# Loading q and k in 32-token blocks and transposing them on VectorE from the third batch on

## The chip, the cores and the metric

The kernel runs on one core of a Trainium2 chip. The metric is the device time of one execution in microseconds (us). Engines are named as in the profile: PE is TensorE's matmuls and PEld its weight loads, DVE is VectorE, ACT is ScalarE, POOL is GpSimd, SP is SyncE, which here only issues DMAs.

## What is computed

For each of 8 batches and 8 heads, 32 pack vectors attend over 576 tokens; then the 576 queries attend over the 32 packed results. The attention output of all heads goes through two matrices with a softplus between them.

```python
scale = 1.0 / np.sqrt(q.shape[-1])           # q, k, v: (8, 8, 576, 64), p: (8, 8, 32, 64)
p_packed = sm_attn(p, k, v)                  # softmax(scale * p k^T) v
out = sm_attn(q, p_packed, p_packed)
x = out.transpose(0, 2, 1, 3).reshape(B * S, H * D)        # (4608, 512)
h = x @ w_in                                 # (512, 2048)
g = np.maximum(h, 0.0) + np.log1p(np.exp(-np.abs(h)))
result = (g @ w_out).astype(np.float32)      # (2048, 512)
```

## The kernel before

The work goes batch by batch. A batch has two groups `g` of four heads each, and its 576 tokens are handled in two halves `c` of 288 columns. The main loop (lines 620 to 671) runs over 128 units: a unit is one batch `b` and one of 16 slices `f` of 128 of the 2048 hidden columns. In each unit PE does `gemm1` (line 497: 12 matmuls into the two halves of `ph`), ACT and DVE make the softplus of it (lines 523 to 528) and split it into two parts `gh` and `gl` (513, 514), and two units later (`LAG`) PE does the second product (`gemm2_tile`, line 541: four tiles `acc` of three matmuls). At a batch's last slice each `acc` is copied by DVE to a tile `o` (550) and stored by SP (556); the last 64 tokens of two batches share a tile `acc_m` with 48 further matmuls. There are two banks for `ph`, so the `gemm1` of the next unit overwrites them as soon as the softplus's last reader, line 528 on DVE, is through.

The attention of batch b+1 is a generator, `attention`, that is stepped 0.56 times after each of a unit's four `gemm2` tiles (`PACE`), so that its pieces lie between the matmuls of batch b. PE's order is as written; a scheduler places the other engines' instructions. The pieces that matter here:

- `load` (112 to 122) brings q, k or v of one batch and group by one DMA of SP into a tile of 96 partitions: partition x holds the six tokens 6x to 6x+5 of each head, runs of 1536 bytes. The pool `ld` has four tiles; a load waits until the tile of four loads before is read to its end.
- `transposed` (234 to 246) turns one head of k or q so that its 64 dimensions lie on the partitions: three transposes on PE into a PSUM bank `psT` (line 239), and one ACT copy of 128 x 288 to the tile `T` (line 245). Two tokens are turned at once, so that rows 0 to 63 of `T` hold the tokens of one half and rows 64 to 127 those of the other. There are 16 such calls in a batch.
- `scores1` and `scores2` (line 252) multiply by `T`; `a1` (261) and `at_h`, `at_l` (442, 443) take the results, the two halves next to each other. So the tokens stand in another order than in memory, the same in all steps; `packed` (295) picks v to match, and `store` undoes it with two DMAs for each tile of 128 rows.
- `scores2`'s result goes through DVE: 32 x 32 transposes (319, 343) around a softmax over 32 columns (lines 327 to 340).

Of the kernel before, what the change touches and what calls it, by code (L numbers as in the profile page):

```python
# [26 lines left out]
def pack_attention_then_softplus_ffn(  # L27
# [10 lines left out]
    nc = tc.nc  # L38
# [13 lines left out]
    LAG = 2  # L52
    MC = 512
# [58 lines left out]
    def load(nm, b, g):  # L112
        if b >= B:
            return
        t = ld.tile([NP, HG, SI, D], F32, tag="ld", name=f"{nm}_{b}_{g}")
        nc.sync.dma_start(
            t.rearrange("x h s d -> x h (s d)"),
            {"q": q, "k": k, "v": v}[nm][b, g * HG:(g + 1) * HG].rearrange(
                "h (x s) d -> x h (s d)", s=SI
            ),  # L120
        )
        loaded[nm, b, g] = t
# [111 lines left out]
    def transposed(nm, b, g, hh):  # L234

        src = loaded[nm, b, g]
        ps = bank(f"psT_{nm}_{b}_{g}_{hh}")
        for i in range(HS):
            nc.tensor.transpose(  # L239
                ps[:, i * NP:(i + 1) * NP],  # L240
                src[:, hh, 2 * i:2 * i + 2, :].rearrange("x s d -> x (s d)"),
                ident[:NP, :NP],
            )
        dst = work.tile([P, C], F32, tag="T", name=f"T_{nm}_{b}_{g}_{hh}", bufs=4)
        nc.scalar.copy(dst, ps[:, :C])  # L245
        return dst
# [10 lines left out]

    def scores1(b, g, c, kT, a1):
        cols = slice(b % BG * J, (b % BG + 1) * J)
        ps = scores(1, b, g, c, lambda hh: pT[:, g * HG + hh, cols], kT)  # L260
        nc.scalar.copy(a1[:, c * C:(c + 1) * C], ps)
# [28 lines left out]
    def packed(b, g, a1T, rs):  # L290

        ps = bank(f"psp_{b}_{g}")
        for s in range(SI):
            for hh in range(HG):
# [3 lines left out]
                    loaded["v", b, g][:, hh, 2 * (s % HS) + s // HS, :],  # L298
# [134 lines left out]
    def weights(b):  # L433
# [4 lines left out]
        for c in range(2):  # L438
            cols = slice(c * C, (c + 1) * C)
            for g in range(G):  # L440
                aT = res[b]["aT"][g, c]
                nc.scalar.copy(at_h[:, g, cols], aT)
                nc.vector.tensor_tensor(  # L443
                    at_l[:, g, cols], aT, at_h[:, g, cols].bitcast(F32), op=ALU.subtract
                )
# [100 lines left out]
    outv = [out[b * S:(b + 1) * S, :].rearrange("(x s) e -> s x e", s=SI) for b in range(B)]  # L546

    def store(acc, pieces, nm):
        o = cv.tile([P, DM], F32, tag="x", name=f"o_{nm}", bufs=2)
        nc.vector.tensor_copy(o, acc)  # L550
        for row, b, col, n in pieces:
            while n:
                i, x = divmod(col, NP)
                m = min(n, NP - x)
                s = i % HS * 2 + i // HS
                nc.sync.dma_start(outv[b][s, x:x + m, :], o[row:row + m, :])
# [144 lines left out]
```

## Time and profile before

| what | value |
|---|---|
| runs of the kernel | 799.79, 796.33 and 799.0 us; median 799.0 |
| profiled execution, first to last instruction (span) | 794.2 us; its own time is not listed beside it |
| PE busy | 766.6 us (97%) |
| DVE busy | 511.3 us (64%) |
| ACT busy | 464.8 us (59%) |
| POOL busy | 94.2 us (12%) |
| DMA queue of SP | 37,600 packets, 54.93 MB, 27.2% of 16 engines |
| chain that ended last | PE 80%, and all else under 1% each |

The span is that of one profiled execution and the runs are others; the median of the runs is 4.8 us above the span, the fastest run 2.1 us. The busy share of an engine is its mean over the span. "Chain" is the work followed back from the last instruction, at each step to what released it.

### The profile page before, as it was taken

Reading aid. Unit: us, or ns where it says so; the run is one execution under the profiler, and the core shown is the slowest. Engines: PE = TensorE matmul, PEld = TensorE weight load, DVE = VectorE, ACT = ScalarE, POOL = GpSimd, SP = SyncE. Lnnn points to the kernel's source line nnn. Section 1 sums busy time; section 2 is a strip of 40 time slices with the busy share of each in tenths; the row PEclk is TensorE's granted clock in tenths of the full one; section 3 lists DMA queues with packets and bytes.
Section 4 is the critical chain, followed back from the end, with each engine's and each line's share of the span. In section 5 each row is a group of like instructions: output and inputs, shape, how many; then the busy total and the mean of one; then the engine's idle time right before and its main releaser. Section 6 shows DMA issues by size and latency. Waiting matters only on the chain.

```text
span 794.2 us, 14986 instructions
## 1 busy us (share of the span) xinstructions
PE 766.6 (97%) x5724; PEld 609.0 (77%) x5724; DVE 511.3 (64%) x1168; ACT 464.8 (59%) x1181; POOL 94.2 (12%) x166
## 2 busy tenths in 40 slices
PE   6879988999999999999999999999999999999997
PEld 4656766877788787877788787887888777778886
DVE  2788899754686547765677447764677546765554
ACT  5769887665662755665554555665555465555540
POOL 1415353000000000000000000000000000000010
PEclk9999999999999999999999999999999999999999
DMA  9977784031213121032213112132211210010002
GB/s 229 248 188 178 172 229 112 8 107 31 61 31 83 45 56 48 18 83 61 61 31 84 26 50 60 31 84 61 61 31 42 56 31 2 1 54 1 1 0 67
DMA packets 38216, 56.02 MB, mean 71 GB/s; under 512 B 4864, under 2 KB 31488, under 8 KB 38144
## 3 DMA queue, kind: packets, MB, share of 16 engines
q1 hardware_dynamic: 37600, 54.93, 27.2%
q8 instruction: 45, 0.74, 0.4%
q14 instruction: 27, 0.22, 0.1%
q10 hardware_dynamic: 544, 0.13, 0.1%
HBM read 45.61 MB, written 9.44 MB: 69 GB/s over the span
## 4 chain that ended last, share of the span: by engine, by line
PE 80%; ACT 0%; DVE 0%; issue 0%; ACTq 0%; DVEq 0%
PE acc L541 40%; PE ph L497 23%; PE acc_m L541 6%; PE psm L460 3%; PE ps L252 2%; PE psT_q L239 2%; PE psT_k L239 2%; PE psp L295 1%; PE psa L285 1%; PE psx L308 0%; PE ppt L105 0%; ACT e L525 0%; ACT e L524 0%; ACT e L523 0%; DVE o L550 0%; DVE o_m L550 0%
## 5 line engine op out<-in xcount | busy, mean ns | idle before, releaser
L528 DVE SCALAR_TENSOR_TENSOR e<-ph,e 128x288 f32<-128x288 f32 x256 | 114.5, 454 | 167.5 <-ACT e L525 166.2
L541 PE MATMUL acc<-wo_h,gh 128*128 128x512 f32 x512 | 214.8, 419 | 0.7 <-DVE o L550 0.7
L541 PE MATMUL acc<-wo_l,gh 128*128 128x512 f32 x512 | 201.6, 394 | 0.0
L541 PE MATMUL acc<-wo_h,gl 128*128 128x512 f32 x512 | 201.5, 394 | 0.0
L523 ACT ACTIVATE e<-ph 128x288 f32<-128x288 f32 x256 | 103.0, 403 | 163.1 <-PE ph L497 110.7
L497 PE MATMUL ph<-at_h,mh 128*128 128x288 f32 x512 | 159.0, 311 | 5.4 <-DVE e L528 4.5
L497 PE MATMUL ph<-at_l,mh 128*128 128x288 f32 x512 | 152.2, 297 | 1.4 <-DVE at_l L443 1.2
L497 PE MATMUL ph<-at_h,ml 128*128 128x288 f32 x512 | 152.2, 297 | 0.0
L497 PEld LDWEIGHTS ph<-at_h,mh 128*128 128x128 f32 x512 | 96.8, 189 | 40.0 <-DVE gl L514 14.1
L534 POOL COPY rest<-e 128x64 f32<-128x64 f32 x128 | 47.3, 369 | 599.3 <-DVE e L528 598.5
L541 PEld LDWEIGHTS acc<-wo_h,gh 128*128 128x128 f32 x512 | 96.4, 188 | 23.1 <-issue 9.8
L541 PEld LDWEIGHTS acc<-wo_h,gl 128*128 128x128 f32 x512 | 96.4, 188 | 21.7
L524 ACT ACTIVATE e<-e 128x288 f32<-128x288 f32 (+1 forms) x240 | 109.2, 455 | 3.5
L525 ACT ACTIVATE e<-e 128x288 f32<-128x288 f32 (+1 forms) x240 | 109.7, 457 | 2.0
L541 PEld LDWEIGHTS acc<-wo_l,gh 128*128 128x128 f32 x512 | 96.9, 189 | 9.8
L497 PEld LDWEIGHTS ph<-at_l,mh 128*128 128x128 f32 x512 | 97.0, 189 | 4.5 <-DVE at_l L443 2.3
L497 PEld LDWEIGHTS ph<-at_h,ml 128*128 128x128 f32 x512 | 96.9, 189 | 0.0
L514 DVE TENSOR_TENSOR gl<-e,gh 128x512 fp32r<-128x512 f32 x128 | 88.0, 688 | 6.9 <-DVE gh L513 0.5
L513 DVE CAST gh<-e 128x512 fp32r<-128x512 f32 x128 | 57.8, 452 | 6.2
L475 ACT CAST mh<-psm 128x512 fp32r<-128x512 f32 (+1 forms) x72 | 35.5, 541 | 41.2 <-PE psm L460 40.8
L476 DVE TENSOR_TENSOR ml<-psm,mh 128x512 fp32r<-128x512 f32 (+1 forms) x72 | 42.7, 622 | 21.8 <-ACT mh L475 21.7
L460 PE MATMUL psm<-w_in_sb,pt 64*32 64x512 f32 (+1 forms) x576 | 38.6, 553 | 6.3 <-ACT T_q L245 2.1
(75 smaller groups left out, 816.7 us busy)
## 6 DMA issues: line engine op xcount, KB each, us to landing
k<-in_k SPq DMA_DIRECT2D x16, 576.0 KB, 4.6
v<-in_v SPq DMA_DIRECT2D x16, 576.0 KB, 4.5
q<-in_q SPq DMA_DIRECT2D x16, 576.0 KB, 4.9
x_i<-in_moe_w_in SPq DMA_DIRECT2D x32, 256.0 KB, 5.9
x_o<-in_moe_w_out SPq DMA_DIRECT2D x16, 512.0 KB, 3.7
out<-o SPq DMA_DIRECT2D x24, 192.0 KB, 2.5
out<-o SPq DMA_DIRECT2D x16, 128.0 KB, 2.4
out<-o SPq DMA_DIRECT2D x24, 64.0 KB, 2.8
```

The costliest lines, as they stand in the source:

```text
L460: nc.tensor.matmul(ps[hh * J:(hh + 1) * J, :n], res["pt"][g][o:o + D, hh * J:(hh + 1) * J], w_in_sb[o:o + D, hh, c * n:(c + 1) * n], start ...
L475: nc.scalar.copy(mh[:, cols], ps[:, :n])
L476: nc.vector.tensor_tensor(ml[:, cols], ps[:, :n], mh[:, cols].bitcast(F32), op=ALU.subtract)
L497: nc.tensor.matmul(ph[:, :C], x[:, ms], y[:, g, cs], start=(i == 0), stop=(i == 3 * G - 1),)
L513: nc.vector.tensor_copy(hi, x)
L514: nc.vector.tensor_tensor(lo, x, hi.bitcast(F32), op=ALU.subtract)
L523: nc.scalar.activation(es[c], hv[c], AF.Abs)
L524: nc.scalar.activation(e[:, x], e[:, x], AF.Exp, scale=-1.0)
L525: nc.scalar.activation(e[:, x], e[:, x], AF.Ln, bias=1.0)
L528: nc.vector.scalar_tensor_tensor(es[c], hv[c], 0.0, es[c], op0=ALU.max, op1=ALU.add)
L534: nc.gpsimd.tensor_copy(rest[:, rest_at(b, f), r:r + REST], e[:, NT * P:])
L541: nc.tensor.matmul(acc, x[:, cs], y[:, f, :], start=(first and i == 0), stop=(last and i == 2),)
```

## The change

The constant `BY_BLOCK` is 2: batches 0 and 1 stay as they are, and batches 2 to 7 keep their tokens in the order of memory. There a tile of q or k has 128 partitions and is loaded by four DMAs, one for 32 partitions each: a partition gets 4 heads x 9 blocks x 32 numbers, and the runs in memory are 32 numbers (128 bytes). Partitions 0 to 63 take the even blocks of 32 tokens, 64 to 127 the odd ones, and two neighbouring groups of 32 partitions the two halves of the 64 dimensions. One VectorE instruction, a transpose of 32 x 32 blocks of the whole 128 x 288, then makes the tile `T` from SBUF; PE's three transposes, the PSUM bank and ACT's copy are gone. A tile of v is loaded by one DMA in runs of 64 numbers (256 bytes) instead of 384 (1536 bytes). The copies to `a1`, `at_h` and `at_l` write blocks of 32 columns with a step of 64 (`half`, `by_half`), and the result of a tile of 128 rows is stored by one DMA.

```diff
--- before.py
+++ after.py
@@ -50,6 +50,8 @@
     NT = S // P
     REST = S - NT * P
     LAG = 2
+    BY_BLOCK = 2
+    NB = C // J
     MC = 512
     scale = 1.0 / math.sqrt(D)
 
@@ -112,13 +114,25 @@
     def load(nm, b, g):
         if b >= B:
             return
-        t = ld.tile([NP, HG, SI, D], F32, tag="ld", name=f"{nm}_{b}_{g}")
-        nc.sync.dma_start(
-            t.rearrange("x h s d -> x h (s d)"),
-            {"q": q, "k": k, "v": v}[nm][b, g * HG:(g + 1) * HG].rearrange(
-                "h (x s) d -> x h (s d)", s=SI
-            ),
-        )
+        src = {"q": q, "k": k, "v": v}[nm][b, g * HG:(g + 1) * HG]
+        if b < BY_BLOCK:
+            t = ld.tile([NP, HG, SI, D], F32, tag="ld", name=f"{nm}_{b}_{g}")
+            nc.sync.dma_start(
+                t.rearrange("x h s d -> x h (s d)"), src.rearrange("h (x s) d -> x h (s d)", s=SI)
+            )
+        elif nm == "v":
+            t = ld.tile([NP, HG, SI, D], F32, tag="ld", name=f"{nm}_{b}_{g}")
+            nc.sync.dma_start(
+                t.rearrange("x h s d -> x (h s) d"), src.rearrange("h (s x) d -> x (h s) d", s=SI)
+            )
+        else:
+            t = ld.tile([P, HG, NB, J], F32, tag="ld", name=f"{nm}_{b}_{g}")
+            blocks = src.rearrange("h (n c x) (w d) -> c w x (h n) d", c=2, x=J, w=D // J)
+            for o in range(P // J):
+                c, w = divmod(o, D // J)
+                nc.sync.dma_start(
+                    t[o * J:(o + 1) * J].rearrange("x h n d -> x (h n) d"), blocks[c, w]
+                )
         loaded[nm, b, g] = t
 
     CN = 512
@@ -234,6 +248,10 @@
     def transposed(nm, b, g, hh):
 
         src = loaded[nm, b, g]
+        if b >= BY_BLOCK:
+            dst = work.tile([P, C], F32, tag="T", name=f"T_{nm}_{b}_{g}_{hh}", bufs=4)
+            nc.vector.transpose(dst, src[:, hh].rearrange("x n d -> x (n d)"))
+            return dst
         ps = bank(f"psT_{nm}_{b}_{g}_{hh}")
         for i in range(HS):
             nc.tensor.transpose(
@@ -255,10 +273,22 @@
             )
         return ps[:, :C]
 
+    def half(b, c, x):
+
+        if b < BY_BLOCK:
+            return x[:, c * C:(c + 1) * C]
+        return x.rearrange("p (n c x) -> p c n x", c=2, x=J)[:, c]
+
+    def by_half(b, x):
+        return x if b < BY_BLOCK else x.rearrange("p (n x) -> p n x", x=J)
+
+    def copy_half(b, c, copy, dst, src):
+        copy(half(b, c, dst), by_half(b, src))
+
     def scores1(b, g, c, kT, a1):
         cols = slice(b % BG * J, (b % BG + 1) * J)
         ps = scores(1, b, g, c, lambda hh: pT[:, g * HG + hh, cols], kT)
-        nc.scalar.copy(a1[:, c * C:(c + 1) * C], ps)
+        copy_half(b, c, nc.scalar.copy, a1, ps)
 
     def softmax1_max(b, g, a1):
         m = small.tile([P, 1], F32, tag="m1", name=f"m1_{b}_{g}", bufs=1)
@@ -295,7 +325,7 @@
                 nc.tensor.matmul(
                     ps[hh * J:(hh + 1) * J, :D],
                     a1T[:, s, hh * J:(hh + 1) * J],
-                    loaded["v", b, g][:, hh, 2 * (s % HS) + s // HS, :],
+                    loaded["v", b, g][:, hh, 2 * (s % HS) + s // HS if b < BY_BLOCK else s, :],
                     start=(s == 0), stop=(s == SI - 1),
                 )
         pp = small.tile([P, 2, D], F32, tag="pp", name=f"pp_{b}_{g}", bufs=1)
@@ -436,12 +466,12 @@
         at_l = work.tile([P, G, S], F32R, tag="at_l", name=f"at_l_{b}", bufs=1)
         res[b]["at"] = (at_h, at_l)
         for c in range(2):
-            cols = slice(c * C, (c + 1) * C)
             for g in range(G):
                 aT = res[b]["aT"][g, c]
-                nc.scalar.copy(at_h[:, g, cols], aT)
+                copy_half(b, c, nc.scalar.copy, at_h[:, g], aT)
                 nc.vector.tensor_tensor(
-                    at_l[:, g, cols], aT, at_h[:, g, cols].bitcast(F32), op=ALU.subtract
+                    half(b, c, at_l[:, g]), by_half(b, aT), half(b, c, at_h[:, g].bitcast(F32)),
+                    op=ALU.subtract,
                 )
 
 
@@ -543,17 +573,24 @@
                 start=(first and i == 0), stop=(last and i == 2),
             )
 
-    outv = [out[b * S:(b + 1) * S, :].rearrange("(x s) e -> s x e", s=SI) for b in range(B)]
+    outb = [out[b * S:(b + 1) * S, :] for b in range(B)]
+
+    def rows_of(b, col):
+
+        if b >= BY_BLOCK:
+            return outb[b][col:]
+        i, x = divmod(col, NP)
+        s = i % HS * 2 + i // HS
+        return outb[b].rearrange("(x s) e -> s x e", s=SI)[s, x:]
 
     def store(acc, pieces, nm):
         o = cv.tile([P, DM], F32, tag="x", name=f"o_{nm}", bufs=2)
         nc.vector.tensor_copy(o, acc)
         for row, b, col, n in pieces:
             while n:
-                i, x = divmod(col, NP)
-                m = min(n, NP - x)
-                s = i % HS * 2 + i // HS
-                nc.sync.dma_start(outv[b][s, x:x + m, :], o[row:row + m, :])
+                to = rows_of(b, col)
+                m = min(n, to.shape[0])
+                nc.sync.dma_start(to[:m], o[row:row + m, :])
                 row, col, n = row + m, col + m, n - m
 
     def rests(b):
```

What moves on DVE, the main loop of batch 4 with the attention of batch 5 in it. In the names, `a_5_0_1` is the second score of batch 5, group 0, half 1; `T_q_1_0` is head 0 of group 1 of q; `e_10` is the softplus of unit 10. Before, from the first transpose of group 0's scores to the softplus of unit 10:

```order
L319 STREAM_TRANSPOSE a_5_0_0_5942<-ps_5_0_0_5937 128x288
L327 TENSOR_REDUCE m_5_0_0_5980<-a_5_0_0_5942 128x9
L319 STREAM_TRANSPOSE a_5_0_1_5949<-ps_5_0_1_5944 128x288
L328 TENSOR_TENSOR a_5_0_0_5942<-a_5_0_0_5942,m_5_0_0_5980 128x288
L327 TENSOR_REDUCE m_5_0_1_6062<-a_5_0_1_5949 128x9
L328 TENSOR_TENSOR a_5_0_1_5949<-a_5_0_1_5949,m_5_0_1_6062 128x288
L336 TENSOR_REDUCE z_5_0_0_5998<-a_5_0_0_5942 128x9
L528 SCALAR_TENSOR_TENSOR e_10_5965<-ph_10_0_5951,e_10_5965 128x288
```

and now:

```order
L349 STREAM_TRANSPOSE a_5_0_0_5748<-ps_5_0_0_5743 128x288
L253 STREAM_TRANSPOSE T_q_1_0_5798<-q_1_5386 128x288
L349 STREAM_TRANSPOSE a_5_0_1_5755<-ps_5_0_1_5750 128x288
L357 TENSOR_REDUCE m_5_0_0_5786<-a_5_0_0_5748 128x9
L253 STREAM_TRANSPOSE T_q_1_1_5858<-q_1_5386 128x288
L358 TENSOR_TENSOR a_5_0_0_5748<-a_5_0_0_5748,m_5_0_0_5786 128x288
L357 TENSOR_REDUCE m_5_0_1_5860<-a_5_0_1_5755 128x9
L253 STREAM_TRANSPOSE T_q_1_2_5871<-q_1_5386 128x288
L558 SCALAR_TENSOR_TENSOR e_10_5771<-ph_10_0_5757,e_10_5771 128x288
```

Three of the four transposes of q's group 1 come in ahead of unit 10's first line 528 (now 558), and two instructions of the softmax have moved behind it.

Further on in the same batch, before, from the second maximum of group 1's scores to unit 13's softplus:

```order
L327 TENSOR_REDUCE m_5_1_1_6188<-a_5_1_1_6142 128x9
L328 TENSOR_TENSOR a_5_1_0_6135<-a_5_1_0_6135,m_5_1_0_6155 128x288
L328 TENSOR_TENSOR a_5_1_1_6142<-a_5_1_1_6142,m_5_1_1_6188 128x288
L336 TENSOR_REDUCE z_5_1_0_6192<-a_5_1_0_6135 128x9
L337 TENSOR_SCALAR z_5_1_0_6192<-z_5_1_0_6192 128x9
L338 RECIPROCAL z_5_1_0_6192<-z_5_1_0_6192 128x9
L339 TENSOR_TENSOR a_5_1_0_6135<-a_5_1_0_6135,z_5_1_0_6192 128x288
L528 SCALAR_TENSOR_TENSOR e_13_6173<-ph_13_0_6159,e_13_6173 128x288
```

and now:

```order
L357 TENSOR_REDUCE m_5_1_1_5978<-a_5_1_1_5932 128x9
L358 TENSOR_TENSOR a_5_1_0_5925<-a_5_1_0_5925,m_5_1_0_5945 128x288
L358 TENSOR_TENSOR a_5_1_1_5932<-a_5_1_1_5932,m_5_1_1_5978 128x288
L253 STREAM_TRANSPOSE T_k_0_0_6146<-k_0_5502 128x288
L366 TENSOR_REDUCE z_5_1_0_5982<-a_5_1_0_5925 128x9
L253 STREAM_TRANSPOSE T_k_0_1_6159<-k_0_5502 128x288
L367 TENSOR_SCALAR z_5_1_0_5982<-z_5_1_0_5982 128x9
L253 STREAM_TRANSPOSE T_k_0_2_6196<-k_0_5502 128x288
L558 SCALAR_TENSOR_TENSOR e_13_5963<-ph_13_0_5949,e_13_5963 128x288
L368 RECIPROCAL z_5_1_0_5982<-z_5_1_0_5982 128x9
L366 TENSOR_REDUCE z_5_1_1_6000<-a_5_1_1_5932 128x9
```

Three of the four transposes of k for batch 6 stand ahead of unit 13's first line 558; the reciprocal and the product with it have moved behind it.

On SP, early in the main loop of batch 4, the stores of batch 3 and the load of q (group 0) for the attention of batch 5, before:

```order
L556 DMA out<-o_0_5286 96x512
L556 DMA out<-o_0_5286 32x512
L556 DMA out<-o_1_5293 64x512 x2
L116 DMA q_0_5425<-in_q 96x4x384
L556 DMA out<-o_2_5307 32x512
L556 DMA out<-o_2_5307 96x512
L556 DMA out<-o_3_5318 96x512
L556 DMA out<-o_3_5318 32x512
```

and now:

```order
L133 DMA q_0_5251<-in_q 32x36x32 x4
L593 DMA out<-o_0_5124 128x512
L593 DMA out<-o_1_5130 128x512
L593 DMA out<-o_2_5139 128x512
L593 DMA out<-o_3_5149 128x512
L593 DMA out<-o_m 64x512 x2
```

The load of q now stands as four DMAs ahead of the stores, where it stood between the second and the third tile, and each tile's store is one DMA.

## Rows read from the trace of the kernel before

**Rows 1.** Busy time by stretch: us, busy by engine (count), PEclk, DMA share, GB/s

```profile
427.00:524.00 97.00, 97.00 (x720) 77.52 (x718) 59.45 (x140) 52.41 (x141) 6.12 (x16) 1.00 0.19 51
524.00:610.00 86.00, 86.00 (x671) 68.53 (x670) 55.32 (x131) 52.22 (x140) 5.94 (x16) 1.00 0.21 55
```

**Rows 2.** Chain of waits from 160 to 700 us, shares by engine and line

```profile
by line: PE acc L541 49.5%; PE ph L497 29.1%; PE acc_m L541 6.1%; PE psm L460 4.5%; PE ps L252 2.9%; PE psT_q L239 2.2%; PE psT_k L239 2.0%; PE psp L295 1.8%; PE psa L285 1.5%; PE psx L308 0.2%; PE ppt L105 0.2%
```

**Rows 3.** Chain of waits from 427 to 524 us in order: start us, us, what

```profile
465.56 0.25 PE psT_q L239 x3
...
487.26 1.39 PE acc L541 x6
...
493.24 0.70 PE acc L541 x3
493.94 0.25 PE psT_q L239 x3
494.19 1.42 PE acc L541 x6
...
495.86 0.73 PE acc L541 x3
496.58 1.59 PE ph L497 x12
...
506.43 1.59 PE ph L497 x12
```

**Rows 4.** Groups, 160 to 700 us: line engine op operands count | busy us, mean ns | idle

```profile
L239 PE MATMUL psT_q<-ident,q 96*128 96x96 f32 x144 | 19.8, 245 | 0.0
...
L245 ACT COPY T_q<-psT_q 128x288 f32<-128x288 f32 x48 | 18.9, 394 | 22.1 <-PE psT_q L239 21.9
...
L239 PE MATMUL psT_k<-ident,k 96*128 96x96 f32 x132 | 18.1, 245 | 0.0
...
L245 ACT COPY T_k<-psT_k 128x288 f32<-128x288 f32 x44 | 17.5, 397 | 23.3 <-PE psT_k L239 22.8
...
L343 DVE STREAM_TRANSPOSE aT<-a 128x288 f32<-128x288 f32 x24 | 11.3, 471 | 0.2
...
L443 DVE TENSOR_TENSOR at_l<-aT,at_h 128x288 fp32r<-128x288 f32 x24 | 10.1, 460 | 0.8
```

**Rows 5.** Busy time in two stretches of 5 us, columns as in rows 1

```profile
489.00:494.00 5.00, 5.00 (x43) 3.44 (x42) 4.96 (x14) 3.39 (x10) 0.24 (x1) 1.00 0.00 0
504.00:509.00 5.00, 5.00 (x28) 4.38 (x27) 4.81 (x15) 3.47 (x11) 0.24 (x1) 1.00 0.02 5
```

**Rows 6.** VectorE in order, 485 to 509 us: start us, us, instruction [idle before <-releaser]

```profile
486.06 0.45 DVE L327 TENSOR_REDUCE m<-a 128x9 f32<-128x288 f32 x1
486.44 0.47 DVE L319 STREAM_TRANSPOSE a<-ps 128x288 f32<-128x288 f32 x1
486.83 0.42 DVE L328 TENSOR_TENSOR a<-a,m 128x288 f32<-128x288 f32 x1
...
494.16 0.46 DVE L528 SCALAR_TENSOR_TENSOR e<-ph,e 128x288 f32<-128x288 f32 x1 [0.15 <-ACT e L525]
495.05 0.46 DVE L528 SCALAR_TENSOR_TENSOR e<-ph,e 128x288 f32<-128x288 f32 x1 [0.44 <-ACT e L525]
...
505.23 0.45 DVE L528 SCALAR_TENSOR_TENSOR e<-ph,e 128x288 f32<-128x288 f32 x1
...
505.98 0.42 DVE L528 SCALAR_TENSOR_TENSOR e<-ph,e 128x288 f32<-128x288 f32 x1
```

**Rows 7.** DMA queue of the four p loads, 133 to 140 us: packets, MB, engine share

```profile
q1 hardware_dynamic: 1088, 0.26, 16.8%
```

**Rows 8.** The same of one v load, 202 to 207 us

```profile
q1 hardware_dynamic: 400, 0.59, 45.3%
```

**Rows 9.** SyncE's DMA issues in order: start us, us, what

```profile
427.31 2.44 SPq L556 DMA_DIRECT2D out<-o  x4
429.84 0.54 SPq L116 DMA_DIRECT2D q<-in_q  x1
```

## The prediction

> **What bounds the kernel now.** I first compared engines by stretch. The reader is to see that in the main loop, with batch 4's 97 us and batch 5's 86 us as examples, PE is busy all of the time at the full granted clock of 1.00 (the 2.4 GHz level), DVE 61 to 64%, ACT 54 to 61%, and the DMA engines about a fifth [rows 1]. The 11 us by which the two batches differ are the 48 matmuls of `acc_m`. Second, the chain of waits between 160 and 700 us: every share belongs to PE, so nothing waits there but for PE's own next matmul, and 4.2% of it are the transposes of q and k at line 239 [rows 2]. Whatever PE no longer has to do in this loop is won, up to the point where another engine comes too late.
>
> **What is removed from PE.** Batches 2 to 7 have 6 x 2 tensors x 2 groups x 4 heads = 96 calls of `transposed`, each three transposes on PE. Between 160 and 700 us there are 144 + 132 of them [rows 4], that is 92 calls; the other four lie shortly before 160. The chain gives 4.2% of 540 us = 22.7 us for 92 calls, 0.247 us each, as its rows in order of time show singly (0.25). All three take 0.25 us although one is listed with 245 ns, because they are pipelined. Around such a piece the matmuls run a little longer: three of `acc` take 0.73 us behind one and 0.70 in front of it, six take 1.42 behind one and 1.39 elsewhere [rows 3]. So a call costs PE 0.25 to 0.30 us; I take 0.27, one such loss of 0.03 being seen most times, though not each time. 96 x 0.27 = **25.9 us** off the path; the ends are 23.7 and 28.8.
>
> **What is removed from ACT.** 96 copies of 128 x 288 at 394 to 397 ns [rows 4], 38 us. ACT is not on the path, so this gives nothing by itself. The softplus's ACT steps come a little earlier, which I don't count.
>
> **What is added to DVE.** 96 transposes of 128 x 288 out of SBUF. The kernel has that very shape at line 343, 471 ns [rows 4]: 45 us in all, 7.5 us for a batch. A batch of 86 us becomes 81.7 (16 x 0.27 less), and DVE's 55.3 us [rows 1] become 62.8, 77%. On average that is covered by PE. It need not be covered in every place: before, DVE already had two dense stretches in each batch, busy 4.96 us of 5 and 4.81 of 5 [rows 5], where the softmax over the packs is done, and the order puts T_q of group 1 into the first and three T_k of the next batch into the second.
>
> In a dense stretch the price is less than 471 ns: instructions of 0.42 to 0.47 us start 0.38 and 0.39 us apart [rows 6], so I take 0.40 for each added one. The one who waits is `gemm1`, which needs a bank of `ph` back from line 528.
> - First stretch. Line 528 of unit 11 ran at 494.16 to 494.62 and 495.05 to 495.51 [rows 6], and unit 12's `gemm1` began at 496.58 [rows 3], its second half 0.79 us on (half of 1.59). Four transposes come ahead of it (1.6 us) and two instructions of 0.40 move behind it, so its first half ends about 0.65 us later (DVE had waited 0.15 there), at 495.3; its second 0.55 later, at 496.1. PE, with three transposes fewer since the stretch began (two of them at 493.94 and just after 494.19's piece), wants the halves at 495.8 and 496.6. Both are in time, by 0.5 us.
> - Second stretch. Unit 13's line 528 ended at 505.68 and 506.40 [rows 6]; unit 14 wanted its banks at 506.43 and 507.22 [rows 3]. Three transposes (1.2 us) come in, a reciprocal and a product move out (about 0.6), so the first half is 0.6 later and the second 0.7: 506.3 and 507.1. PE has no transpose in this stretch to lose and is not earlier. In time by 0.1 us.
>
> That is too near for six batches without a miss. I take 0.2 us a batch, **1.2 us**; the ends are 0, and 8 x 0.47 = 3.8 us a batch or 22.6 us, if all that lies in the two stretches is passed on to PE.
>
> The Trainium skill says otherwise of the 0.40: "VectorE: DVE Perf Modes", section "The DRAIN you can't avoid", has the next instruction start only when the pipe is empty, though it points to cases that start earlier. The starts in rows 6 lie inside the instruction before them, so the trace does not agree here. By that rule each added transpose would cost its whole 0.47 us, the second stretch would miss by 0.1 us and the first not at all, and the sum would be worse by under 1 us.
>
> **What is added to the DMA engines.** A tile of q or k was 384 packets of 1536 bytes and becomes 4 x 32 x 36 = 4608 of 128; a tile of v becomes 96 x 24 = 2304 of 256. No row has a 128-byte packet. The nearest are the loads of p, 256 bytes: 1088 packets took 16.8% of 16 engines in 7 us, 17.3 ns each [rows 7]. I take that as the price, a packet of half the size hardly costing more; half of it (8.6) is the lower end. The upper end is the 1536-byte packet: 400 packets (16 of them small) in 45.3% of 16 engines over 5 us, 90.6 ns [rows 8]. A batch then has 4 x 4608 / 16 = 1152 small and 288 middle packets for each engine: 1440 x 17.3 ns = 24.9 us (15.0 at the lower end), where 144 x 90.6 ns = 13.0 us stood. DMA share goes from about 0.2 to a little over 0.3. The cover is time: q issued at 429.84 [rows 9] is first read at 465.56 [rows 3], 36 us later, and a tile now needs 288 x 17.3 ns = 5.0 us of the engines instead of 2.2.
>
> SP issues 12 more DMAs a batch for loads and about 4 fewer for stores, at 0.54 us for a load [rows 9]: under 5 us of SP in 82, which only issues. The q load that now stands ahead of the stores waits for the transposes of k, which stand on DVE before that batch's last softplus, ahead of the first copy to `o`; it is out before a store is due. The strided copies keep their element counts, and I cost them at nothing; behind them `at_l` (0.46 us each) [rows 4] feeds the first `gemm1` of a batch, so if they were slower, a batch would pay it four times over.
>
> **Sum.** 794.2 - 25.9 + 1.2 = 769.5 us of span. The median lies 4.8 us above that span, so 774 us, 3.1% less. A measurement of this kernel can tell about 0.5%, 4 us.
>
> **Rivals.**
> 1. *DVE comes too late in the dense stretches.* For it: 4.96 of 5 us busy, and a margin of 0.1 us in the second. Against it: margins of about half a microsecond in the first, and units between the two where DVE has time to catch up. Half of the worst case gives 11 us back, 785 us; all of it 22.6, 796 us.
> 2. *The small packets bind, and the kernel is slower.* The place is every load of batches 2 to 7. The engines have some 87 us a batch (the mean of 81.7 and 92.7); with 5.0 us for v and some 4.5 for stores and the rest, the q and k loads bind from (87 - 9.5) / 1152 = 67 ns a packet, and the kernel is slower than before only above 71 ns, where a batch passes 91.5. At the upper end of 90.6 ns a batch takes 114 us, 22 more than before, six times: 799 + 134 = 933 us. Against it: 256-byte packets at 17.3 ns. The Trainium skill's "DMA: Bandwidth & Descriptors", section "Specifications", asks for at least 512 bytes for line rate and names a read-modify-write below; the 256-byte rows show 14.8 bytes a nanosecond and the 1536-byte ones 17.0, so the trace shows little of that at 256 bytes, and no row shows 128.
> 3. *The change does not do what it says*: excluded, the order has 96 transposes on DVE more and 96 ACT copies fewer.
>
> **How the numbers follow.** The forecast, 767 to 780 us, has 0.66. Rival 1 has 0.26, of which 0.20 stay under 795 us and 0.06 end within 4 us of before. Rival 2 has 0.08. So faster 0.86, same 0.06, slower 0.08. The range runs from 768 (28.8 us saved, nothing lost, and a median 2 us nearer to the span, would give 768) to 787, just past half of rival 1's worst case; it leaves out the rest of that rival and rival 2.
>
> **What would show it.** Right: between 160 and 700 us PE still busy throughout, line 239's share of the chain gone with no other name in its place, 96 DVE transposes of about 0.47 us, a batch of about 82 or 93 us, and q and k landing within 10 us. Rival 1: PE idle before `ph` with DVE's line 558 as the releaser, once or twice a batch. Rival 2: DVE waiting at its T transposes for a DMA, the DMA share near 1. The forecast is wrong if the batches shrink by less than 3 us.

## The result and the profile after

| kernel | median of the runs (lowest to highest) | profiled span |
|---|---|---|
| before, on the same chip | 799.39 us (796.33 to 805.64, 4 runs) | 794.2 us |
| after | 791.28 us (789.83 to 792.74, 4 runs) | 789.2 us |

The ratio is 0.9891, 95% interval 0.9848 to 0.9935: faster by about 1.1%, where 3.1% were forecast. The 791.3 us lie 4 us above the upper end of the forecast's range.

I read the time after in two pieces, cut at the first store of batch 0. The stores are in the list of SyncE's issues; the one of batch 0 starts at 157.44 us before and at 176.70 us after. From there to the end of the span it was 794.2 - 157.44 = 636.8 us and is 789.2 - 176.70 = 612.5 us: **24.3 us won in the loop**, where the forecast had 25.9 - 1.2 = 24.7. Up to there **19.3 us were lost**, of which the forecast has nothing. Each of the two pieces is read from one execution, and that of the kernel before is among its fastest: a later run of it with the same span of 794.2 us took 796.02 us, 3.4 us under the median. By the medians 8.1 us are won in all, so that of the 24.3 some 16 are lost ahead of the first store.

The loop first. Batches 4 and 5 again, from first store to first store, with the columns of [rows 1]:

```profile
434.75:527.62 92.87, 92.64 (x671) 73.77 (x670) 62.94 (x156) 47.35 (x125) 6.01 (x16) 1.00 0.27 53
527.62:609.62 82.00, 81.76 (x623) 64.78 (x622) 59.07 (x147) 47.35 (x125) 5.82 (x16) 1.00 0.29 57
```

What were 97 and 86 us are 92.87 and 82.00. PE is as full as before, the clock is at 1.00, DVE has 16 instructions more in a batch, ACT 16 fewer.

The chain of waits between 180 and 700 us, which answers to [rows 2], and the waits of PE from 180 us to the end (waited for: us in total, times, longest):

```profile
by line: PE acc L571 48.4%; PE ph L527 29.7%; PE acc_m L571 6.3%; PE psm L490 4.7%; PE ps L270 2.9%; PE psp L325 1.9%; PE psa L315 1.5%; DVE at_l L472 1.2%; ACT e L554 0.7%; ACT e L553 0.7%; DMA out<-o 0.6%; DVE e L558 0.4%; ACT e L555 0.3%
```

```profile
PE ph L527 <- DVE at_l L472: 1.2, 5, 0.2
PE acc L571 <- DVE o L588: 0.4, 1, 0.4
```

Line 239 (257 now) has left the chain. What came in its place is small. The shares of DVE and ACT are one piece in each batch: in batch 4 the chain goes from 516.2 to 520.1 us through the softplus on ACT, `at_h` and `at_l`. PE works through nearly all of it and waits 0.23 us at its end, for `at_l` at the first `gemm1` of a batch, in five batches. Before, PE had no such wait in the loop. It never waits for line 558, the softplus's last reader, in the two dense stretches.

The wait for `at_l` does not come from DVE's transposes. DVE makes `at_l` in four pieces, two for each half `c`. Here are the last three of them and PE's first matmul that reads `at_l`, before and after (start us, us, instruction):

```profile
515.82 1.23 DVE L443 TENSOR_TENSOR at_l<-aT,at_h 128x288 fp32r<-128x288 f32 x3
516.29 0.29 PE L497 MATMUL ph<-at_l,mh 128*128 128x288 f32 x1
```

```profile
519.20 1.23 DVE L472 TENSOR_TENSOR at_l<-aT,at_h 128x288 fp32r<-128x288 f32 x3
520.11 0.40 PE L527 MATMUL ph<-at_l,mh 128*128 128x288 f32 x1 [0.23 <-DVE at_l L472]
```

DVE is no later than it was: its first piece starts 3.36 us behind the `gemm1` of the unit before in both traces (515.08 behind 511.72, 518.46 behind 515.10). But before, the first 288 columns were half 0 alone, and PE began right behind the second piece, 0.39 us ahead of the third one's end. Now the halves lie in alternating blocks of 32 columns, the first 288 columns hold both, and PE begins 0.05 us behind the end of the third piece. The block-wise copies cost this wait.

The groups that answer to [rows 4], and the DMA queue while nothing but eight k loads was under way, from 464.5 to 474 us (packets, MB, share of 16 engines), which answers to [rows 7, 8]:

```profile
L253 DVE STREAM_TRANSPOSE T_q<-q 128x288 f32<-128x288 f32 x48 | 21.3, 459 | 0.0
L253 DVE STREAM_TRANSPOSE T_k<-k 128x288 f32<-128x288 f32 x44 | 20.2, 469 | 0.0
...
L472 DVE TENSOR_TENSOR at_l<-aT,at_h 128x288 fp32r<-128x288 f32 x24 | 10.1, 462 | 0.8
```

```profile
q1 hardware_dynamic: 9337, 1.18, 79.0%
```

A transpose on DVE takes 0.46 to 0.47 us. A 128-byte packet takes 9.5 us x 16 x 0.79 / 9337 = 12.9 ns.

Now batch 0. Waits of PE from 80 to 180 us, and three stretches of 10 us:

```profile
PE psm L490 <- POOL w_in_sb L207: 20.6, 3, 15.5
PE psm L490 <- ACT a1T L316: 1.9, 1, 1.9
PE ph L527 <- DVE e L558: 0.3, 1, 0.3
```

```profile
130.00:140.00 10.00, 6.27 (x47) 4.47 (x45) 8.37 (x20) 5.75 (x11) 1.80 (x3) 0.96 0.31 73
140.00:150.00 10.00, 0.00 (x0) 0.00 (x0) 8.85 (x24) 4.42 (x8) 2.83 (x2) 0.50 0.57 131
150.00:160.00 10.00, 8.21 (x49) 6.85 (x50) 5.31 (x11) 5.33 (x12) 2.84 (x3) 0.68 0.67 129
```

The first row is the loss: three waits for converted input weights, one of them 15.5 us. The kernel before has no such wait in the same stretch:

```profile
PE psm L460 <- ACT T_q L245: 2.1, 1, 2.1
PE ph L497 <- DVE e L528: 1.7, 2, 1.0
PE psm L460 <- DVE a L319: 1.4, 1, 1.4
PE psm L460 <- DVE pp L303: 0.5, 1, 0.5
```

From 140 to 150 us PE does nothing at all and its granted clock is 0.50, that is the level of 1.2 GHz; behind the wait the first twelve matmuls of `gemm1` take 3.1 us (152.83 to 155.9) instead of 1.6.

What PE waits for there can be followed upwards through four engines: SP's issues, ACT (both start us, us, instruction), POOL and PE.

```profile
120.48 2.45 SPq L145 DMA_DIRECT2D x_o<-in_moe_w_out  x2
122.99 0.42 SPq L125 DMA_DIRECT2D v<-in_v  x1
135.56 3.10 SPq L145 DMA_DIRECT2D x_i<-in_moe_w_in  x4
```

```profile
132.84 0.69 ACT L554 ACTIVATE e<-e 128x576 f32<-128x576 f32 x1
...
134.30 0.67 ACT L188 ACTIVATE m<-x_o 128x512 f32<-128x512 f32 x1
134.87 1.22 ACT L192 ACTIVATE r<-x_o 128x512 int32<-128x512 uint32 x2
136.72 0.67 ACT L188 ACTIVATE m<-x_o 128x512 f32<-128x512 f32 x1 [0.63 <-DVE t L199]
...
144.10 0.64 ACT L188 ACTIVATE m<-x_i 128x512 f32<-128x512 f32 x1
```

```profile
148.03 1.27 POOL L207 TENSOR_TENSOR w_in_sb<-t,r 128x512 int32<-128x512 int32 x1 [6.43 <-DVE t L199]
150.47 1.27 POOL L207 TENSOR_TENSOR w_in_sb<-t,r 128x512 int32<-128x512 int32 x1 [1.16 <-DVE t L199]
```

```profile
135.87 0.40 PE L571 MATMUL acc<-wo_h,gl 128*128 128x512 f32 x1
151.79 1.11 PE L490 MATMUL psm<-w_in_sb,pt 64*32 64x256 f32 x16 [15.52 <-POOL w_in_sb L207]
```

Two `x_o` tiles are asked for at 120.48 and take 5.4 us, so they are there at about 126. ACT converts them at 134.30, eight us later. Only then are their slots free, SP asks for the next `x_i` at 135.56, ACT has it at 144.10, POOL adds it up at 148.03 and 150.47, and PE goes on at 151.79. In the kernel before, the same `x_i` is asked for at 113.92 and POOL is through with it at 128.9:

```profile
106.72 4.34 SPq L131 DMA_DIRECT2D x_o<-in_moe_w_out  x2
112.67 0.66 ACT L174 ACTIVATE m<-x_o 128x512 f32<-128x512 f32 x1
113.92 3.89 SPq L131 DMA_DIRECT2D x_i<-in_moe_w_in  x4
127.33 1.61 POOL L193 TENSOR_TENSOR w_in_sb<-t,r 128x512 int32<-128x512 int32 x1 [1.51 <-ACT r L178]
```

The eight us on ACT are not all of the delay: the two `x_o` tiles are themselves asked for 13.8 us later than before (120.48 against 106.72), so the chain had fallen behind earlier in batch 0. ACT was not overloaded in between, with 5.75 and 4.42 us busy of 10 in the stretches above. It had been given another order, by the scheduler that places all engines but PE. Here are its rows between the first steps of units 10 and 13, of the kernel before and of the change, as the built programs have them (`m` and `r` are the two halves of a weight conversion, `e` the softplus; rows that are in both are left out but for `e` and `mh`):

```
before                                       after
L523 ACTIVATE e_10_1537<-ph_10_1_1530        L553 ACTIVATE e_10_1543<-ph_10_1_1536
L174 ACTIVATE m_1491<-x_o_1409               L188 ACTIVATE m_1483<-x_i_1362
L178 ACTIVATE r_1493<-x_o_1409               L192 ACTIVATE r_1485<-x_i_1362
L178 ACTIVATE r_1551<-x_o_1483               L505 CAST mh_6_0_1622<-psm_6_1_1613
L174 ACTIVATE m_1549<-x_o_1483               L553 ACTIVATE e_11_1642<-ph_11_1_1635
L475 CAST mh_6_0_1616<-psm_6_1_1607          L553 ACTIVATE e_12_1715<-ph_12_1_1708
L523 ACTIVATE e_11_1636<-ph_11_1_1629        L188 ACTIVATE m_1497<-x_o_1415
L174 ACTIVATE m_1590<-x_i_1497               L192 ACTIVATE r_1499<-x_o_1415
L178 ACTIVATE r_1592<-x_i_1497               L192 ACTIVATE r_1557<-x_o_1489
L174 ACTIVATE m_1662<-x_i_1555               L188 ACTIVATE m_1555<-x_o_1489
L178 ACTIVATE r_1664<-x_i_1555               L188 ACTIVATE m_1596<-x_i_1503
L523 ACTIVATE e_12_1709<-ph_12_1_1702        L192 ACTIVATE r_1598<-x_i_1503
                                             L188 ACTIVATE m_1668<-x_i_1561
                                             L192 ACTIVATE r_1670<-x_i_1561
```

Before, each of the units 10 and 11 is followed by two conversions. After, none stands behind unit 11, and all four stand behind unit 12. That this order is the cause, and not a companion of slower loads, is what the experiments are about.

### The profile page after: what moved, and what is told of

It is laid out like the page before. It is cut to its first block, busy times and chain, and to the rows that moved or that the text cites. A ratio compares the mean times of both kernels' runs of the same rounds, so it can differ in the third digit from the quotient of the medians.

```text
span 789.2 us, 14442 instructions
## 1 busy us (share of the span) xinstructions
PE 744.0 (94%) x5436; PEld 589.1 (75%) x5436; DVE 532.9 (68%) x1264; ACT 436.5 (55%) x1085; POOL 91.2 (12%) x166
## 4 chain that ended last, share of the span: by engine, by line
PE 75%; DVE 1%; ACT 1%; DMA 0%; issue 0%; ACTq 0%; DVEq 0%
PE acc L571 38%; PE ph L527 23%; PE acc_m L571 6%; PE psm L490 3%; PE ps L270 2%; PE psp L325 1%; PE psa L315 1%; DVE at_l L472 1%; ACT e L554 0%; ACT e L553 0%; DMA out<-o 0%; DVE e L558 0%; ACT e L555 0%; ACT at_h L286 0%; PE psx L338 0%
## 5 line engine op out<-in xcount | busy, mean ns | idle before, releaser
L571 PE MATMUL acc<-wo_h,gh 128*128 128x512 f32 x512 | 208.1, 407 | 0.4 <-DVE o L588 0.4
L571 PEld LDWEIGHTS acc<-wo_h,gl 128*128 128x128 f32 x512 | 96.3, 188 | 21.6
L490 PE MATMUL psm<-w_in_sb,pt 64*32 64x512 f32 (+1 forms) x576 | 39.4, 569 | 23.5 <-POOL w_in_sb L207 20.6
L543 DVE CAST gh<-e 128x512 fp32r<-128x512 f32 x128 | 56.2, 439 | 5.8
```

The lines of the kernel that those rows point to most:

```text
L490: nc.tensor.matmul(ps[hh * J:(hh + 1) * J, :n], res["pt"][g][o:o + D, hh * J:(hh + 1) * J], w_in_sb[o:o + D, hh, c * n:(c + 1) * n], start ...
L543: nc.vector.tensor_copy(hi, x)
L571: nc.tensor.matmul(acc, x[:, cs], y[:, f, :], start=(first and i == 0), stop=(last and i == 2),)
```

## The experiments

In each profile I took the start of `gh` (one DVE cast for each unit) in units 0 and 15 of batch 0. The difference leaves out what varies ahead of unit 0, where the runs lie between 53.3 and 59.1 us. "Order of batch 0" is what the built program has on ACT.

| run | order of batch 0 | loads of batch 2's k | units 0 to 15 | first store | median | ratio to before (95%) |
|---|---|---|---|---|---|---|
| before | - | 1 DMA, 1536 B | 96.9 us | 157.44 | 799.39 | - |
| after | late | 4 DMAs, 128 B | 115.0 | 176.70 | 791.28 | 0.9891 (0.9848 to 0.9935) |
| e1 | changed, not late | behind the weights | 99.8 | 159.76 | 779.90 | 0.9746 (0.9717 to 0.9775) |
| e2 | as before | 1 DMA, 1536 B | 99.3 | 162.85 | 779.60 | 0.9742 (0.9710 to 0.9775) |
| e3 | half as late | 4 DMAs, 4608 B | 110.6 | 171.32 | 785.97 | 0.9819 (0.9784 to 0.9853) |
| e4 | ACT early | 4 DMAs, 128 B | 113.0 | 174.45 | 790.35 | 0.9874 (0.9840 to 0.9909) |
| e5 | partly late | 1 DMA, 128 B | 105.7 | 167.19 | 807.38 | 1.0130 (1.0085 to 1.0174) |
| e6 | as e1 | as e1 | 98.9 | 162.76 | 810.00 | 1.0134 (1.0100 to 1.0169) |
| e8 | late | 4 DMAs, 128 B | 117.0 | 178.16 | 791.76 | 0.9915 (0.9886 to 0.9945) |
| e9 | ACT early | 4 DMAs, 128 B | 113.1 | 178.90 | 789.25 | 0.9891 (0.9847 to 0.9935) |
| e10 | ACT by unit as before | 4 DMAs, 128 B | 123.7 | 183.99 | 796.14 | 0.9981 (0.9961 to 1.0001) |
| e11 | the same, k pinned | 4 DMAs, 128 B | 119.2 | 179.51 | 793.00 | 0.9939 (0.9920 to 0.9959) |
| e12 | ACT by unit as after | 1 DMA, 1536 B | 108.9 | 175.02 | 809.99 | 1.0140 (1.0109 to 1.0171) |
| e13 | all engines as before | 4 DMAs, 128 B | 101.2 | 162.58 | 777.32 | 0.9718 (0.9684 to 0.9752) |
| e14 | all engines as after | 1 DMA, 1536 B | 115.7 | 177.85 | 816.05 | 1.0201 (1.0160 to 1.0241) |

**Where the loss sits: e1 and e2.** e1 collects the k and v loads of batch 2 and issues them behind the last weight load; e2 leaves batch 2 as it was and changes batches 3 to 7 only.

```diff
+        if b == BY_BLOCK and nm != "q" and not now:
+            late.append((nm, b, g))
+            return
...
+            if (b, f) == (0, 14):
+                with tc.issue_after(lastx[-1].ins):
+                    for x in late:
+                        load(*x, now=True)
```

```diff
-    BY_BLOCK = 2
+    BY_BLOCK = 3
```

Expected of e1: 

> The changed kernel with one thing moved: the loads of k and v for batch 2 (the only small-packet loads that are issued while the weights are still being loaded and converted in batch 0) stand on SyncE behind the last weight load. All three theories of the loss in batch 0 (order: the scheduler has put the conversion of the last weights later on ScalarE and VectorE, and PE waits for w_in_sb; queue: a k load that waits for PE stands ahead of weight loads on SyncE; packets: the 128-byte packets take the DMA engines from the weight loads) expect 772 to 777 us, with the first store at about 157 to 160 us and PE's wait for w_in_sb under 3 us. If the loss has nothing to do with those loads: 791 us. If the steady loop's gain is not the 24 us that the two traces show, 785 us or more with the wait for w_in_sb gone.

Expected of e2: 

> The changed kernel with BY_BLOCK = 3: batch 2 is loaded and transposed as before, and only batches 3 to 7 in the new way. Nothing in batch 0 then differs from the kernel before. Of 24.3 us gained behind the first store, five sixths remain: 799.4 - 20.3 = 779 us (777 to 782). If the gain is not even over the batches, another number; if the loss came from the later batches, about 790 us.

Both are 2.5% faster than before, e2 as forecast, e1 3 us above its range: it took 88.8 us from the first store of batch 0 to that of batch 1, where 82 were due. PE waits 3.7 us there for a copy `o` that stands behind batch 2's transposes on DVE. The long wait for `w_in_sb` is gone in both. So the loss comes with the loads of batch 2 that are issued in batch 0; e1 moved k and v together and does not tell them apart. e2 is a control as well: its batch 0 stands on every engine as before, and its first store still came 5.4 us later, 3.0 of them ahead of unit 0. So much a single profile of the same instructions can differ.

**Runs, packets or the queue: e3, e5, e8.** e3 loads k of batch 2 by four DMAs in runs of 4608 bytes; the tile then holds other numbers. e5 is the kernel before with one DMA of 128-byte runs for q and k from batch 2 on; these hold their numbers in another order. e8 keeps the k loads of batch 2 at their place in the program on SP.

In e5, on the kernel before:

```diff
+        if b >= 2 and nm != "v":
+            nc.sync.dma_start(
+                t.rearrange("x h s d -> x (h s d)").rearrange("x (n d) -> x n d", d=32),
...
+                    "(n x d) -> x n d", x=NP, d=32
```

In e8, on the changed kernel:

```diff
-                nc.sync.dma_start(
+                x = nc.sync.dma_start(
...
+                if (nm, b) == ("k", BY_BLOCK):
+                    tc.keep_in_program_order(x)
```

Expected of e3: 

> The changed kernel in which k of batch 2 (both groups) is loaded by the same four DMAs of 32 partitions each, but in runs of 4608 bytes, so that batch 2's k holds other numbers than it should. Its DMA count and place in SyncE's queue stay. Packets: the loss in batch 0 goes, 772 to 777 us. Order and queue: SyncE's order is as in the changed kernel and the weights' conversion still stands late on ScalarE, 784 to 792 us, with PE waiting over 8 us for w_in_sb.

Expected of e5: 

> The kernel before, with q and k of batches 2 to 7 loaded by one DMA each in 128-byte runs (they hold the numbers in another order); PE's transposes and ACT's copies stay. Same number of packets as the change, no more DMAs. Cover (the small packets are hidden in the loop): the periods of 86 and 97 us stay within 0.5 us, 797 to 803 us. Packets: batch 0's first store later by 5 us or more for two tiles of k, 803 us or more; if they bind in the loop, 820 or more.

Expected of e8: 

> The changed kernel, but the k loads of batch 2 keep their place in the program on SP (group 1's first DMA no longer stands ahead of three weight loads); all packets stay as they are, and ACT's order is left to the scheduler. Queue (the k load that waits for PE holds up the weight loads, and this alone costs the 19 us): first store near 160 us, 775 to 781 us. Packets (the 128-byte packets take the DMA engines from the weight loads): as changed, 786 to 791 us. Order (ACT's late weight conversions): 786 to 791 us too, the conversions behind unit 11 stay in one lump ahead of unit 12. If loads and conversions each suffice to be late: 783 to 789 us.

e8 refutes the queue: the k load no longer stands ahead of three weight loads, and nothing is won. e3 and e5 seem to say that four DMAs cost some 14 us and small packets some 9. But the scheduler had rearranged batch 0 in both, by part of what it did in the change, so they mix the load and the order. What e5 does show is the loop: its batches 3 to 5 take 86.01, 96.95 and 86.03 us where the kernel before has 86.0 and 97.0. There the small packets cost nothing.

**Pins on ACT that settled nothing: e4, e9, e10, e11.** e4 makes ACT do each conversion as early as the program has it, e9 adds e8's pin, e10 puts the last conversions ahead of the units where the kernel before has them, e11 adds e8's pin to that.

In e10:

```diff
+    CONV_BY = {7: 19, 8: 21, 9: 24, 10: 25, 11: 27, 12: 29, 13: 31}
...
+                        with tc.issue_after(conv_m[n].ins), tc.issue_after(conv_r[n].ins):
+                            nc.scalar.activation(es[c], hv[c], AF.Abs)
```

Expected of e4: 

> The changed kernel with ScalarE's order alone pinned in batch 0: a unit's first softplus instruction may not stand ahead of a weight conversion that the program has before it. The loads, their packets and their place on SyncE stay as they are. Order: PE's wait for w_in_sb falls from 20.6 us to under 6 and the time to 773 to 780 us. Queue: the first DMA of k for batch 2, group 1, still waits 5 us for PE ahead of the weights, so 8 us or more of the loss stay, 783 to 791 us. Packets: 789 to 793 us.

Expected of e9: 

> Both pins together: k loads of batch 2 in program order on SP, and ACT's weight conversions of batch 0 in program order. Same packets. Packets theory: PE still waits for w_in_sb, first store later than 168 us, 784 to 790 us. Queue or queue and ACT order together: first store near 160 us, 773 to 781 us. The ACT pin alone took 1 us, so if this one is under 781 and the SP pin alone is over 785, it takes both.

Expected of e10: 

> The changed kernel, all its loads as they are, but in batch 0 ACT is made to do the last 12 weight conversions ahead of the same units as in the kernel before. Order theory, sharpened (the order of ACT, not the loads, makes the weights late: in the changed kernel five conversions stand behind unit 12's first step, where the kernel before has them ahead of units 11 and 12): first store at 157 to 164 us, 773 to 780 us. Packets or queue (the weight tiles themselves land too late): ACT then waits for them, first store 170 or later, 785 to 792 us.

Expected of e11: 

> The run before, and the k loads of batch 2 keep their place in the program on SP as well. Order alone: like the run before within 2 us. Queue as a second cause: 3 us or more faster than the run before. Packets: 785 to 792 us.

In all four the wait for `w_in_sb` shrank, to between 3.6 and 6.5 us where the change has 20.6, and none was clearly faster than the change for it: PE waited 12.5 to 15.1 us for the softplus on DVE instead, where the change waits 0.3. So e4 has the short wait that the order theory expected, and not the time. By its text e10, with a first store far behind 170 us, spoke for the loads, and I nearly took it so. ACT in e11, the same with the k loads in place (start us, us, instruction, idle time before it):

```profile
100.64 0.40 ACT L267 COPY T_q<-psT_q 128x288 f32<-128x288 f32 x1 [4.01 <-PE psT_q L261]
104.01 0.40 ACT L267 COPY T_q<-psT_q 128x288 f32<-128x288 f32 x1 [2.96 <-PE psT_q L261]
104.31 0.66 ACT L192 ACTIVATE m<-x_i 128x512 f32<-128x512 f32 x1
```

The `x_i` tile had been issued at 91.82 and such a load takes under 5 us, so it was there at about 97. Its conversion came at 104.31, because the scheduler had put two `T_q` copies ahead of it, each waiting for PE, and ACT idled 7 us. A pin of a few instructions on one engine had moved others. To hold the order, all of it has to be held.

**The order alone, and the loads alone: e12, e13, e14.** e12 puts the last six conversions of the kernel before where the change has them on ACT. e13 and e14 are exact. e13 is the changed kernel, with all instructions of ACT, DVE, POOL and SP that are written ahead of batch 2's attention, some 620, in the order of the kernel before (PE's order agrees anyway); e14 is the kernel before in the order of the changed one.

In e13 and e14, each with its own table:

```diff
+    ORDER = {
+        "Activation": """
...
+    for row in ORDER.values():
+        ids = [f"I-{x}" for x in row.split()]
+        for x, y in zip(ids, ids[1:]):
+            tc.add_manual_dep(
+                traced[y], x,
...
```

Expected of e12: 

> The kernel before, no small packet and no DVE transpose in it, with its last six weight conversions put behind unit 12's (one behind unit 13's) first ACT step, where the changed kernel has them. Order theory: PE waits 10 to 20 us for w_in_sb ahead of unit 14, first store 168 to 178 us, 810 to 820 us. Packets or queue: ACT has the time, first store 157 to 163, 797 to 804 us.

Expected of e13: 

> The changed kernel, all its loads and DVE's transposes as they are, with the instructions of batch 0 on ACT, DVE, POOL and SP held in the very order in which the kernel before has them (the four DMAs of a k load at the place of its one). Order theory (the new loads made the scheduler rearrange batch 0, and the arrangement costs the 19 us): first store at 157 to 164 us, 773 to 780 us. Loads theory (the k loads themselves make the weight tiles late on the chip, by SP's time or the DMA engines'): first store 170 us or later, 784 us or more.

Expected of e14: 

> The kernel before, its loads and PE transposes as they are, with the instructions of batch 0 on ACT, DVE, POOL and SP in the order that the changed kernel has (a k load at the place of the first of its four DMAs). Order theory: first store 170 to 180 us, PE waits 10 us or more for w_in_sb, 812 to 820 us. Loads theory: first store 157 to 166 us, 797 to 806 us.

All three fell where the order theory had them, e12 at the lower edge of its range. Waits of PE from 80 to 180 us in e13, and SP's issues in the same stretch:

```profile
PE psm L490 <- ACT T_q L263: 3.5, 1, 3.5
PE ph L527 <- DVE e L558: 2.1, 2, 1.3
PE psm L490 <- ACT a1T L316: 1.9, 1, 1.9
PE psm L490 <- DVE a L349: 1.4, 1, 1.4
...
```

```profile
88.50 3.11 SPq L133 DMA_DIRECT2D k<-in_k  x4
91.74 3.06 SPq L145 DMA_DIRECT2D x_i<-in_moe_w_in  x4
...
107.70 3.92 SPq L133 DMA_DIRECT2D k<-in_k  x4
...
117.53 5.21 SPq L145 DMA_DIRECT2D x_i<-in_moe_w_in  x4
```

The four DMAs and the small packets are all there, twice four k DMAs of 3.1 and 3.9 us on SP, and no wait for `w_in_sb` is left. And the same waits in e14, with ACT at the place that was shown above of the changed kernel:

```profile
PE psm L460 <- POOL w_in_sb L193: 20.0, 3, 14.9
PE psm L460 <- ACT a1T L286: 1.8, 1, 1.8
PE ph L497 <- DVE e L528: 0.3, 1, 0.3
```

```profile
135.16 0.67 ACT L174 ACTIVATE m<-x_o 128x512 f32<-128x512 f32 x1
...
144.96 0.64 ACT L174 ACTIVATE m<-x_i 128x512 f32<-128x512 f32 x1
```

Without one small packet and without a transpose on DVE, e14 repeats the change's batch 0 within a microsecond: waits of 20.0 us for `w_in_sb` where the change has 20.6, the late conversion at 135.16 where the change has 134.30, units 0 to 15 in 115.7 us where the change has 115.0. Its two `x_o` tiles are asked for at 120.50, as late as the change's at 120.48. So the order costs 14 to 19 us by itself. With the old loads it is 115.7 less the kernel before's 96.9 or e2's 99.3, and by the medians 816.05 - 799.49 = 16.6. With the new loads it is 115.0 - 101.2 = 13.8, and by the medians 791.28 - 777.32 = 14.0. This is shown, in both directions. The new loads with the order held make 101.2 of 96.9 or 99.3, that is 1.9 to 4.3 us; the two numbers that they are compared with differ by 2.4 on the same instructions, so whether the loads cost anything by themselves stays open. Why the scheduler chose that order was not tried apart: it arranged batch 0 anew with each form of the k load (e3, e5), changed it in e1 too, where units 0 to 15 take 99.8 us and nothing came late, and left it alone in e2.

e13 is also the fastest version, 777.3 us, 2.8% under the kernel before and inside the forecast's 767 to 780; its interval overlaps those of e1 and e2, so among the three no order is claimed.

**What PE's transposes cost: e6.** e1 with the three transposes of each call kept on PE, into a bank that nobody reads; DVE still makes `T`.

```diff
             nc.vector.transpose(dst, src[:, hh].rearrange("x n d -> x (n d)"))
+            ps = bank(f"psT_{nm}_{b}_{g}_{hh}")
+            for i in range(HS):
+                nc.tensor.transpose(
...
```

Expected: 

> The first experiment's kernel (late loads) with PE's three transposes per call kept, unread, into a bank. 96 calls at the forecast's 0.27 us (0.25 to 0.30): 24 to 29 us slower than the first experiment's 779.9, 804 to 809 us, all of it in the loop, periods of about 86 and 97 us again. If DVE's transposes hid a loss of their own that PE's covers, it would be less, 795 to 803 us.

It is 810.0 us, 30.1 more than e1 and 1 us above its range. The first stores from batch 1 on lie 97.85, 86.60, 97.51, 86.61 and 96.92 us apart, in e1 93.42, 81.97, 92.86, 81.97 and 92.86. That is 4.06 to 4.65 us a batch, 0.25 to 0.29 us a call, and some 27 us in six batches. The other 3 us of the 30 lie ahead of unit 0, where e6's profile is 3.3 us later than e1's.

## Why the prediction missed

- **PE's transposes.** Forecast 0.27 us a call, between 0.25 and 0.30. The periods shrank by 4.08 and 4.02 us; with the new wait of 0.23 us that is 4.28 / 16 = 0.268 us. e6 has 0.25 to 0.29. Right.
- **ACT's copies**, forecast at nothing: right, PE waits for ACT nowhere in the loop.
- **DVE's transposes.** Forecast 1.2 us in all, from the dense stretches; in the loop PE lost nothing to them that a wait shows. It never waits for line 558, so the margins were enough, and rival 1 did not come. DVE's busy time rose by 3.5 and 3.8 us a batch (59.45 to 62.94, 55.32 to 59.07), half of the 7.5 that was forecast. The instruction behind a transpose still starts inside it, at 0.40 and 0.39 us of 0.47:

```profile
533.40 0.47 DVE L253 STREAM_TRANSPOSE T_k<-k 128x288 f32<-128x288 f32 x1
533.80 0.11 DVE L297 TENSOR_SCALAR nm<-m 128x1 f32<-128x1 f32 x1
...
534.16 0.47 DVE L253 STREAM_TRANSPOSE T_k<-k 128x288 f32<-128x288 f32 x1
534.55 0.65 DVE L544 TENSOR_TENSOR gl<-e,gh 128x512 fp32r<-128x512 f32 x1
```

  The rule of the Trainium skill's "VectorE: DVE Perf Modes", section "The DRAIN you can't avoid", by which it starts at the end of the one before, is not what these rows show; the section itself says that some instructions start earlier.
- **The strided copies**, costed at nothing: wrong by 1.2 us. They take no longer (`at_l` 462 ns after 460), but the first `gemm1` of a batch now needs three pieces of `at_l` where it needed two, and waits 0.23 us in five batches. e6 has this wait too, with PE's transposes back; e5, with the old copies, does not. That it comes to the 1.2 us forecast for the transposes is luck.
- **Small packets.** Forecast 17.3 ns with ends of 8.6 and 90.6; it is 12.9 ns. Rival 2 needed 67. DMA share is 0.27 and 0.29, a little less than the "little over 0.3". The rate falls to 128 / 12.9 = 9.9 bytes a nanosecond, against 17.0 in [rows 8]: the penalty for short runs that the Trainium skill's "DMA: Bandwidth & Descriptors" names in "Specifications" is there, and at this share of the queue nothing waits for it.
- **SP's issues** were forecast at 0.54 us each; the eight k DMAs of a batch take 6.7 to 7.7 us from first to last, 0.84 to 0.96 each with the pause between the two tiles in it. In the loop that hides too.
- **The step that failed** is the one that costed the new loads at nothing: "The cover is time", with its q that is read 36 us after its issue, and "under 5 us of SP in 82, which only issues". The cover itself held where it was read, in the loop. But it was taken for all six batches, and the step asked only for the time of the loads, not for the order that the scheduler makes around them. The loads of batch 2 are issued in batch 0, among the weight loads, where ACT, DVE and POOL still convert weights and each conversion frees the slot of a later load. No row of that stretch was read for the step, and the order of the changed program was looked at in the dense stretches alone. With the new order PE waits 20.6 us for converted weights, and that order costs 16 to 19 us even without the new loads (e14); with the old order the new loads add 1.9 to 4.3 by the profiles, which may be nothing (e13). ACT's order in batch 0, shown above, has the late conversions in plain sight: those of `x_o` stand two units later. In the trace of the kernel before, unit 10's `gh` starts at 119.1 us and unit 12's at 134.0, so an estimate of 14.9 us for this move was there to be read. It is a rough one: e12, which moves ACT's last six conversions and nothing else by hand, took 9.6 to 12.0 us more in units 0 to 15 (108.9 against 99.3 or 96.9).
- **The median.** The forecast put it 4.8 us above the span; after the change it lies 2.1 above. With 2.1 the forecast would have been 771.6 us and the miss larger, so this error hid a part of the other. It also helps e13 into the forecast's range: its span of 776.5 us is 7 us above the forecast's 769.5.
- **The rivals.** None had this. The sum was right for the loop, and the kernel is faster, though by a third of what was forecast: of 24.3 us won, 19.3 by the two profiles and some 16 by the medians were given back before the first store.

## What to carry to other kernels

Where a scheduler places the instructions, a changed load can also be a changed order, on engines that the change does not touch; compare the order in the prologue too, above all where a chain of load, conversion and slot has no slack. To tell an order from the load that brought it about, hold the whole order of all engines, in both directions: pins on one engine moved other instructions, and four runs of that kind settled nothing. A term that is costed at nothing by a loop's rows has to be costed once more in the batch where that loop is not yet running.

## What was not expected of the hardware

A 128-byte packet costs 60 to 75% of a 256-byte one: 12.9 ns, against 17.3 in [rows 7] and 7 us x 16 x 0.447 / 2320 = 21.6 ns for one v load alone in the queue, between 483 and 490 us in the change. And profiles that run the same instructions up to unit 0 reach it between 53.3 and 59.1 us, a spread that is wider than the 4 us which the medians can tell apart; so batch 0 was compared from unit 0 on.
